# Two-layer attention and GEGLU kernel with a planned instruction order: last unit in two parts of keys, fillers near both ends, new constants per stretch

## The chip, the cores and the metric

The kernel runs on one NeuronCore of one Trainium2 chip. The metric is the device time in microseconds (us), the median of the runs shown. There are five engines with queues of their own: TensorE (PE, matmuls; its weight loads are a separate row, PEld), VectorE (DVE), ScalarE (ACT), GpSimd (POOL) and SyncE (SP, which only issues DMAs here). SBUF is the working memory, PSUM the accumulators: 8 banks of 512 fp32 columns on 128 partitions.

## The reference

Two rounds of the same two layers, on x of 2048 tokens by 512, in bfloat16. LN is a layernorm without parameters, H = 32 heads of 16:

```python
x = x + A(LN(x));  x = x + B(LN(x));  x = x + A(LN(x));  x = x + B(LN(x))
# A: q, k, v = split_heads(x @ wqkv)
#    o = softmax(q @ k.T * 16 ** -0.5) @ v ;  merge_heads(o) @ wo
# B: (gelu_tanh(x @ w_gate) * (x @ w_up)) @ w_down      # w_gate, w_up: 512 x 1792
```

## The kernel before, in words

Everything stays in SBUF between load and store. Queries are worked in blocks, 512,512,512,512 in the first layer and 512,512,512,256,256 in the second (`layer_blocks`). A *unit* is one block for one group of 4 heads, so there are 8 units per block. For each unit:

- **Phase 1** (`p1_emit`, matmul L1507): scores of 128 queries by 512 keys for one head, four heads in four row groups of the array; DVE reduces each such tile, or two banks at once, to the row maximum (L1522, banks 0 to 3). Some tiles are *folded*: a matmul against a difference of two key blocks, an ACT relu (L1334), and one DVE operation (L1517) do two tiles in one. `fin` makes the negative maximum of all keys, transposes it (L897, L899), and `negmax` puts it by four small DMAs (L916, SP's queue) into a spare row of the query tile in `QT`, so that the second matmul has the maximum already subtracted.
- **Phase 2** (`p2_emit`, matmul L1378): scores again, transposed, 512 columns a tile. ACT takes the exponential (L1354) out of banks 4 to 6 (also 3 in the wide mode), two banks at once (128x1024, a *pair*) or one (128x512, a *single*), into a slot of `SCR`. Then the products with V (`pv_emit`, L1402) accumulate in bank 7; `nrm` divides by the sum.
- Beside these run the projections and the feed-forward (L651), transposes (L749), their evictions (L666 DVE, L668 ACT), out-projection with the residual (L979 DVE or L984 ACT + POOL), gelu (L1091 ACT), the up product (L1104 DVE or L1110 ACT + POOL), and the last sum and store (L1130).

The order on every engine is fixed when the program is built. A planner keeps a reckoned clock for each engine (`clk`) and, at each step of PE, takes phase 1, phase 2, products, or other work (`chains`, by due time). Its choices hang on 19 constants that change every 16 steps of phase 1 (`PLAN`, one line of constants per stretch, 129 lines). Three matter for reading the change:

- `NT`: how many banks of phase 2 are issued in one go. `P2B`: whether phase 2 outside the wide mode may use a pair: 0 singles only (banks 4, 5, 6), 1 a pair in 4 and 5 and a single in 6, 2 pairs at 4 or 5. `LAG`: how far phase 2 may trail phase 1 before the wide mode.
- Fillers: `warm_emit` (L1544) issues a matmul of zeros, 240 columns, whose result nobody reads. [...]

The first three units of the second layer (`split`) are worked in two parts already: exponentials of 12 of 16 key tiles with the maximum of those keys, kept (`keep_part`), scaled by exp of the difference of the maxima, and added to the rest (`nrm`).

The last unit of all is an ordinary one before: its `nrm` takes the quick path (L941, L943), straight out of bank 7. After it come the out-projection of the last 256 rows, their layernorm (`ln_fast`), their feed-forward and the store; the other engines have nothing else left then.

Of the kernel before, what the change touches and what calls it, by code (L numbers as in the profile page):

```python
# [6 lines left out]
BF = mybir.dt.bfloat16  # L7
F32 = mybir.dt.float32
# [12 lines left out]
PLAN = [  # L21
# [289 lines left out]
def _build(nc, x_in, wqkv, wo, wg, wu, wd, out, layer_blocks=((512, 512, 512, 512), (512, 512, 512, 256, 256)),  # L311
# [16 lines left out]
    with es:  # L328
# [267 lines left out]
        for la in range(1, NL):  # L596
            for i, u in enumerate([u for u in range(NU) if units[u][0] == la][:NSPL]):
                assert units[u][3] == 512 and i < n_pre
                split[u] = i
# [1169 lines left out]
```

## Time and profile before

| | |
|---|---|
| median of 3 runs | 2550.32 us (2549.87 to 2550.61) |
| the profiled execution: its own time | 2550.05 us |
| its span, first to last instruction | 2548.3 us |
| busy in the span | PE 2450.2, DVE 2423.5, ACT 2356.9, POOL 589.6 us |
| granted PE clock, mean | 0.999 |

Three views are used. The page gives busy time per engine, the chain of waits that ended last, and groups of instructions (count, busy us, mean ns of one, then idle time of the engine in front of them and what ended it). The windows give busy time of every engine between two times, then the granted clock and the DMA share. The timeline gives runs of equal instructions in order, with the idle time in front of them in square brackets.

### The profile page before, as it was taken

The page shows a single profiled execution, that of the slowest core. Times are in us where ns is not written, and L with a number is a line of the kernel's source. Part 1 is how long each engine was busy: PE and PEld are TensorE (multiplying, and loading weights), DVE is VectorE, ACT ScalarE, POOL GpSimd, SP SyncE. Part 2 cuts the span into 40 slices and gives each one's busy share as a digit, 9 for nine tenths or more (in the row PEclk, how much of TensorE's full clock was granted, in tenths as well). Part 3 has the DMA queues.
Part 4 walks back from the last instruction along what each step waited for, and adds up shares of the span by engine and source line. Part 5 has one row for each costly group of instructions (what it writes and reads, how often), then busy time and mean ns, then how long its engine had stood idle before and what let it go on. Part 6 is the DMA issues. An engine that isn't in the chain of part 4 may idle for free.

```text
span 2548.3 us, 67924 instructions
## 1 busy us (share of the span) xinstructions
PE 2450.2 (96%) x29939; PEld 1166.4 (46%) x29939; DVE 2423.5 (95%) x3191; ACT 2356.9 (92%) x3111; POOL 589.6 (23%) x722
## 2 busy tenths in 40 slices
PE   7999999999999999999999999999999999999998
PEld 3444443444434454444434455444543445544555
DVE  7999999999999999999998999999999999999993
ACT  7899998999989999999979899999998999989996
POOL 4010123311133213421133211241113211341200
PEclk9999999999999999999999999999999999999999
DMA  3110000000000000000000000000000000000000
GB/s 100 38 56 6 4 8 2 4 2 2 8 2 4 4 2 6 4 2 16 10 5 4 12 2 4 8 4 8 5 8 1 6 6 3 4 3 12 3 7 6
DMA packets 27367, 25.04 MB, mean 10 GB/s; under 512 B 9408, under 2 KB 26048, under 8 KB 27072
## 3 DMA queue, kind: packets, MB, share of 16 engines
q1 hardware_dynamic: 27072, 20.71, 2.8%
q8 instruction: 234, 3.83, 0.6%
q14 instruction: 61, 0.50, 0.1%
HBM read 9.70 MB, written 2.10 MB: 5 GB/s over the span
## 4 chain that ended last, share of the span: by engine, by line
PE 43%; ACT 32%; DVE 23%; issue 1%; POOL 0%; POOLq 0%; ACTq 0%
ACT SCR L1354 29%; DVE PM L1522 22%; PE PS L1507 14%; PE PS L651 12%; PE PS L1402 9%; PE PS L1378 4%; PE PS L1544 4%; ACT SCR L1334 1%; DVE SCR L1517 1%; PE PS L1327 1%; PE PS L749 0%; ACT XNT L668 0%; ACT SG L668 0%; ACT AO L984 0%; ACT ACCS L948 0%
## 5 line engine op out<-in xcount | busy, mean ns | idle before, releaser
L1522 DVE TENSOR_REDUCE PM<-PS 128x1 f32<-128x512 f32 (+1 forms) x2492 | 2207.6, 948 | 56.2 <-PE PS L1378 27.8
L1354 ACT ACTIVATE SCR<-PS 128x1024 bf16<-128x1024 f32 (+1 forms) x2385 | 2002.7, 931 | 72.4 <-PE PS L1378 51.2
L1507 PE MATMUL PS<-KT,QT 32*128 32x512 bf16 x3914 | 1008.2, 384 | 40.0 <-DVE PM L1522 25.2
L1378 PE MATMUL PS<-QT,KT 32*128 32x512 bf16 (+1 forms) x4608 | 926.3, 360 | 14.0 <-ACT SCR L1354 11.9
L1402 PE MATMUL PS<-VP,SCR 128*128 128x51 bf16 (+1 forms) x16384 | 808.9, 187 | 18.2 <-ACT SCR L1354 13.3
L1402 PEld LDWEIGHTS PS<-VP,SCR 128*128 128x128 bf16 x16384 | 571.0, 96 | 509.7 <-issue 427.1
L1507 PEld LDWEIGHTS PS<-KT,QT 32*128 32x128 bf16 x3914 | 240.8, 91 | 514.7 <-DVE PM L1522 298.2
L1544 PE MATMUL PS<-WV,ZER 128*128 128x240 bf16 x2483 | 432.3, 266 | 4.1 <-ACT SCR L1354 4.1
L966 POOL TENSOR_TENSOR RL<-ACCS,CM 128x16 f32<-128x16 f32 (+1 forms) x63 | 173.4, 2753 | 1032.8 <-ACT ACCS L948 1032.5
L1378 PEld LDWEIGHTS PS<-QT,KT 32*128 32x128 bf16 x4608 | 228.9, 91 | 85.7 <-ACT SCR L1354 62.5
L1544 PEld LDWEIGHTS PS<-WV,ZER 128*128 128x128 bf16 x2483 | 189.0, 96 | 67.9 <-issue 53.9
L1112 POOL TENSOR_TENSOR HT<-HT,AO 128x512 bf16<-128x512 bf16 (+1 forms) x109 | 121.2, 1113 | 273.7 <-ACT AO L1110 273.7
L651 PE MATMUL PS<-WD,HT 128*128 128x512 bf16 x448 | 130.6, 381 | 0.1
L651 PE MATMUL PS<-XNT,WU 128*128 128x512 bf16 (+1 forms) x504 | 127.6, 357 | 0.0
L1517 DVE CUSTOM_DVE_ANT_0 SCR<-PS,SCR 128x512 bf16<-128x512 f32 x182 | 118.0, 685 | 6.0 <-PE PS L1507 2.3
L1149 POOL TENSOR_TENSOR KD<-KT 128x512 bf16<-128x512 bf16 x71 | 81.9, 1154 | 176.1 <-PE PS L1327 162.2
L651 PE MATMUL PS<-XNT,WG 128*128 128x512 bf16 (+1 forms) x504 | 119.4, 359 | 1.3 <-ACT HT L1091 0.9
L1091 ACT ACTIVATE HT<-PS 128x512 bf16<-128x512 f32 (+1 forms) x126 | 69.1, 550 | 50.5 <-PE PS L651 49.5
L1334 ACT ACTIVATE SCR<-PS 128x1024 bf16<-128x1024 f32 (+1 forms) x116 | 99.3, 856 | 16.1 <-PE PS L1327 15.6
L986 POOL TENSOR_TENSOR X<-X,AO 128x512 f32<-128x512 f32 x46 | 58.3, 1268 | 197.2 <-ACT AO L984 197.0
L1110 ACT ACTIVATE AO<-PS 128x512 f32<-128x512 f32 (+1 forms) x109 | 63.8, 585 | 0.4
L651 PEld LDWEIGHTS PS<-XNT,WG 128*128 128x128 bf16 x504 | 39.2, 98 | 53.5 <-issue 29.3
(99 smaller groups left out, 884.9 us busy)
## 6 DMA issues: line engine op xcount, KB each, us to landing
KT<-SG SPq DMA_DIRECT2D x64, 64.0 KB
QT<-MT SPq DMA_DIRECT2D x236, 1.0 KB
QT<-SG SPq DMA_DIRECT2D x56, 64.0 KB
out_dram<-AO SPq DMA_DIRECT2D x16, 128.0 KB, 1.7
WG<-in_B_w_gate_dram SPq DMA_DIRECT2D x4, 448.0 KB, 5.1
WU<-in_B_w_up_dram SPq DMA_DIRECT2D x4, 448.0 KB, 4.8
WD<-in_B_w_down_dram SPq DMA_DIRECT2D x4, 384.0 KB, 4.9
SCR<-in_A_x_dram SPq DMA_DIRECT2D x2, 512.0 KB, 5.4
```

What stands on the lines that cost most here:

```text
L651: ins = e.matmul(out_ap, lhsT=l, rhs=r_, start=(i == 0), stop=(i == n - 1))
L966: emit("pool", lambda e: e.tensor_tensor(RL[:, s, 0:4 * nq], lsum, CM1[:, 0:4 * nq], op=ALU.pow), r=[("ACCS", s), ("CM1",)], w=[("RL", s)] ...
L1112: emit("pool", lambda e, ft=ft, o=o: e.tensor_tensor(HT[:, ft, 0:n], HT[:, ft, 0:n], AO[:, o, 0:n], op=ALU.mult), r=[("AO", o), ("HT", ft) ...
L1149: emit("pool", lambda e: e.tensor_tensor(KD[:, s, :], KT[:, g, ka * 512:(ka + 1) * 512], KT[:, g, kb * 512:(kb + 1) * 512], op=ALU.subtrac ...
L1334: emit("act", lambda e: e.activation(PT[:, s0:s0 + cnt, :], PS[:, bk:bk + cnt, :], ACTF.Relu), r=bks, w=[("PT", s0 + d) for d in range(cnt ...
L1354: emit("act", lambda e: e.activation(dst, src, ACTF.Exp, scale=DH ** -0.5), r=[BK[bk + i] for i in range(cnt)], w=[("PT", i) for i in slot ...
L1378: ins = e.matmul(bank(bk)[:, i * n:(i + 1) * n], lhsT=KT[32 * j:32 * j + 32, g, kt * 128:(kt + 1) * 128], rhs=QT[32 * j:32 * j + 32, s, 0: ...
L1402: ins = e.matmul(acc, lhsT=PT[:, slot, i * n + qt * 128:i * n + (qt + 1) * 128], rhs=AP(VP, (kt * H + 4 * g + j) * 17, [[NTT * H * 17, 128 ...
L1507: ins = e.matmul(bank(b), lhsT=QT[32 * j:32 * j + 32, s, qt * 128:(qt + 1) * 128], rhs=KT[32 * j:32 * j + 32, g, kb * 512:(kb + 1) * 512], ...
L1517: emit("dve", lambda e, i=i, b=b, sl=sl: e.tensor_tensor_reduce(PT[:, sl, :], bank(b), PT[:, sl, :], 1.0, -3.0e38, ALU.add, ALU.max, po[:, ...
L1522: emit("dve", lambda e: e.tensor_reduce(po, PS[:, bs[0]:bs[0] + cnt, :], axis=AX.X, op=ALU.max), r=bks, w=[("PM", sm) + h[1:] for h in hs] ...
L1544: return e.matmul(PS[:, b, NACC:512], lhsT=ZER[:, :], rhs=WV[:, 0, 0:512 - NACC], start=(b != 7), stop=(b != 7), skip_group_check=True)
```

## The change

- **PLAN**: 120 of the 129 lines of constants differ. `NT` is 3 in 39 lines (11 before), `P2B` is 0 in 24 (8 before).
- **TSPL**: the last unit (256 queries) goes into `split` too: part one is keys 0 to 1535 (`TNA` = 3 of 4 blocks), part two the rest. Its phase 1 list is sorted by part. The first part has a query tile of its own (`q_copy`, POOL) with the partial maximum; `keep_part`, the scale (`merge`) and one DVE addition in `nrm` join the parts. The same switch for the first unit (HSPL) is off.
- **merge**: the scaling of a kept part, which stood in `nrm`, becomes a chain of its own that may run earlier; phase 1 of the unit six later also waits for it.
- **TW**: once no phase 2 and no products are left, fillers are wanted up to an occupancy of 0.95 instead of 0.55.
- **HF**: in the first 60 us of the planner's clock, from 12 us on, gaps of PE are filled with fillers whatever the occupancy.

Counted in the two programs' order: PE fillers 2483 to 2408; exponentials: pairs 1711 to 1575, singles 674 to 946; relus of folds: pairs 66 to 53, singles 50 to 79; folds 182 to 185; DVE maxima: pairs 1240 to 1237, singles 1252 in both.

```diff
 PLAN = [
-    (0.0, 0.15, 0.45, 0.42, 0.3, -0.05, 1, 1, 62, 84, 8, 60, 0.3, 2.0, 0, 2, 2, 2, 7),
+    (0.0, 0.25, 0.45, 0.42, 0.3, -0.05, 1, 1, 70, 84, 8, 60, 0.3, 2.0, 0, 2, 2, 2, 7),
...
-NSPL=3, VS=14,
+NSPL=3, HSPL=0, TSPL=1, HNA=3, TNA=3, HV=16, TW=0.95, HF=60, VS=14,
...
+        if TSPL:
+            assert units[NU - 1][3] <= 256
+            split[NU - 1] = NSPL
+            n_part[NU - 1] = TNA
+            extra[NU - 1] = NU % n_qt
+            tail = [h for h in p1_list if h[0] == NU - 1]
+            p1_list[len(p1_list) - len(tail):] = [h for h in tail if h[2] < TNA] + [h for h in tail if h[2] >= TNA]
...
+        def merge(u):
...
+            yield ("cond", lambda: u in kept and u in fin_rec and gel["on"] is None)
+            yield ("pool", [("MSEL", s1), ("MSB", i)], [("DW", i)])
+            emit("pool", lambda e: e.tensor_tensor(DW[:, i, 0:4 * nq], sgn[0], sgn[1], op=ALU.subtract),
...
+            yield ("act", [("DW", i)], [("DW", i)])
+            emit("act", lambda e: e.activation(DW[:, i, 0:4 * nq], DW[:, i, 0:4 * nq], ACTF.Exp, scale=DH ** -0.5),
...
+            emit("pool", lambda e: e.tensor_tensor(pv, pv, wv, op=ALU.mult),
...
+        def q_copy(u):
...
+            emit("pool", lambda e: e.tensor_copy(QT[:, s2, 0:n], QT[:, sl, 0:n]), ...
...
         def nrm(u):
...
             if FAST and (SF or la == NL - 1) and t0 + n == S and g == NG - 1:
+                src, src_t, src_o, keys = PS, 8 * 512, 7 * 512, [BK[7]]
+                if u in split:
+                    av = ACCS[:, s, 0:na].rearrange("p (a b) -> p a b", a=nq)
+                    emit("dve", lambda e: e.tensor_tensor(av, PS[:, 7, 0:na].rearrange("p (a b) -> p a b", a=nq), pa, op=ALU.add),
+                         r=[BK[7]] + pk, w=[("ACCS", s)], dur=0.1 + 0.067 * nq)
+                    src, src_t, src_o, keys = ACCS, 2 * NACC, s * NACC, [("ACCS", s)]
...
-            if u >= n_ahead and u - n_ahead not in qp2_rec:
+            if u >= n_ahead and (u - n_ahead not in qp2_rec or u - n_ahead in split and u - n_ahead not in merged):
                 return None
...
             want, must = (WARM + BOOST, WARML + BOOST / 2) if ahead else (WARM, WARML)
+            if TW and p2["u"] >= NU and not pvq:
+                want = must = TW
             cool = load < want and now > 12 and warm_bank(now) is not None
...
+            if HF > now > 12 and mode[0] == "full" and est(r=[("WV",)], w=[BK[7]]) <= now:
+                for _ in range(int((tn - now - 0.1) / 0.105)):
+                    sch.op("pe", warm_fn(7), r=[("ZER",), ("WV",)], w=[BK[7]])
             clk["pe"] = max(now + 0.01, tn)
```

More of the change, by code (lines that the diff above doesn't have):

```diff
@@ L595, in _build @@
         split = {}
+        n_part = {}
+        extra = {}
         for la in range(1, NL):
@@ L599, in _build @@
                 split[u] = i
+                n_part[u] = NKB - 1
+        if HSPL:
+            split[0] = 0
+            n_part[0] = HNA
+            extra[0] = n_qt - 1
+        if TSPL:
[5 more added lines that the diff above has]
+            p1_list[len(p1_list) - len(tail):] = [h for h in tail if h[2] < TNA] + [h for h in tail if h[2] >= TNA]
         seq = []
@@ L603, in _build @@
                 seq.append((u, 2))
-            elif split[u] == 0:
-                seq += [(v, pt) for pt in (0, 1) for v in sorted(split) if units[v][0] == units[u][0]]
+            elif split[u] in (0, NSPL):
+                seq += [(v, pt) for pt in (0, 1) for v in sorted(split) if v == u or u not in extra and units[v][0] == units[u][0] and v not in extra]
         first_p1 = {}
@@ L614, in _build @@
         p1_left = {u: 16 * units[u][3] // 128 for u in range(NU)}
-        p1_part = {u: 12 * units[u][3] // 128 for u in split}
+        p1_part = {u: 4 * n_part[u] * units[u][3] // 128 for u in split}
         part_rec = set()
         part_done = set()
+        copied = set()
+        kept = set()
+        merged = set()
+        merges = {}
         pair = {u: (2, 3) if u == 0 else (0, 1) for u in range(NU)}
@@ L839, in qproj @@
                 yield ("cond", lambda: u + 1 - n_qt in p2_done)
+            if 0 in extra and u + 1 == extra[0]:
+                yield ("cond", lambda: 0 in part_done)
             tts = range(t0 // 128, (t0 + n) // 128)
@@ L854, in fn @@
                     return ins
-                emit("sp", fn, r=[("SG", s), ("ZER",)], w=keys, grp="sd%d" % (2 * s + i), nd=2 if u + i >= n_qt else 1, dur=0.3)
+                emit("sp", fn, r=[("SG", s), ("ZER",)], w=keys, grp="sd%d" % (2 * s + i), nd=2 if u + i >= n_qt or 0 in extra and u + i == extra[0] else 1, dur=0.3)
                 qt1_rec.add(u + i)
@@ L906, in negmax @@
             s1 = u % n_ahead
-            sl = u % n_qt
+            sl = extra[u] if part and u in extra else u % n_qt
             nq = units[u][3] // 128
-            if u in split and not part:
+            if u in extra:
+                yield ("cond", lambda: u in copied)
+            elif u in split and not part:
                 yield ("cond", lambda: u in part_done)
@@ L925, in part_out @@
             i = split[u]
+            if i == NSPL:
+                return ATT[:, 2:2 + units[u][3] // 128, 0:136].bitcast(F32), [("ATTX",)]
             lo = (0, 192, 328)[i]
@@ L1180, in _build @@
         for la in range(NL):
+            u0 = min(u for u in range(NU) if units[u][0] == la)
             for b in range(NKB):
@@ L1188, in _build @@
                     due = first_k[(la, 2 * c, b)] - KD_
-                    if b == NKB - 1 and any(units[u][0] == la and units[u][4] // 2 == c for u in split):
-                        due = min(due, blk_end[units[min(split)][1] - 1] + VS - 1)
+                    if b == NKB - 1 and la and any(units[u][0] == la and units[u][4] // 2 == c for u in split if u not in extra):
+                        due = min(due, blk_end[units[u0][1] - 1] + VS - 1)
                     add(kproj(la, c, b), due, True)
-            u0 = min(u for u in range(NU) if units[u][0] == la)
             for tt in range(NTT):
-                if u0 in split:
+                if u0 in split and u0 not in extra:
                     add(vproj(la, tt), blk_end[units[u0][1] - 1] + VS)
                 else:
-                    add(vproj(la, tt), last_p1[u0] + VD + 2 * tt)
+                    add(vproj(la, tt), last_p1[u0] + VD + 2 * tt - (HV if u0 in extra and tt < 4 * n_part[u0] else 0))
             for bi, (bl, qi, t0, n) in enumerate(blocks):
@@ L1208, in _build @@
                 add(qproj(u), first_p1[u] - QD, True)
+        for u in extra:
+            add(q_copy(u), first_p1[u])
         if FMAX:
@@ L1216, in _build, with kgs @@
         pvq = []
-        part_kg = {0: (0, NTT - 4), 1: (NTT - 4, NTT)}
-        pv_left = {(u, pt): 4 * (NTT if pt == 2 else part_kg[pt][1] - part_kg[pt][0]) * units[u][3] // 512 for u, pt in seq}
+        def kgs(u, pt):
+            a = 4 * n_part[u] if pt < 2 else 0
+            m = 512 // units[u][3]
+            return list(range(a // m if pt == 1 else 0, a // m if pt == 0 else NTT // m))
+        pv_left = {(u, pt): 4 * len(kgs(u, pt)) for u, pt in seq}
         pv_first = set(seq)
@@ L1224, in p2_group @@
                 return None
-            if seq[p2["i"]][1] == 0 and any(vp_rec.get(kt) != units[u][0] for kt in range(NTT - 4)):
+            if seq[p2["i"]][1] == 0 and any(vp_rec.get(kt) != units[u][0] for kt in range(4 * n_part[u])):
                 return None
@@ L1228, in p2_group, with q_slot @@
                 pt = seq[p2["i"]][1]
-                p2["todo"] = [list(range(*part_kg[pt]) if pt < 2 else range(NTT * units[u][3] // 512)) for j in range(4)]
+                p2["todo"] = [kgs(u, pt) for j in range(4)]
             return u
+        def q_slot(u):
+            return extra[u] if u in extra and seq[p2["i"]][1] == 0 else u % n_qt
         def p2_left():
@@ L1277, in f_head @@
             u = i[0]
-            if u not in kd_rec or u not in qt1_rec or (u >= n_ahead and u - n_ahead not in qp2_rec):
+            if u not in kd_rec or u not in qt1_rec or (u >= n_ahead and (u - n_ahead not in qp2_rec or u - n_ahead in split and u - n_ahead not in merged)):
                 return None
@@ L1449, in p1_skip @@
                 p1_left[u] -= 1
-                if u in split:
+                if u in split and p1_list[pos["g"]][2] < n_part[u]:
                     p1_part[u] -= 1
+                    assert p1_part[u]
                 pos["p1"] += 0.5
@@ L1463, in p1_plan @@
                 return None
-            if u >= n_ahead and u - n_ahead not in qp2_rec:
+            if u >= n_ahead and (u - n_ahead not in qp2_rec or u - n_ahead in split and u - n_ahead not in merged):
                 return None
-            if u in split and kb == NKB - 1 and u not in part_rec:
+            if u in split and u not in extra and kb >= n_part[u] and u not in part_rec:
                 return None
@@ L1526, in p1_emit @@
             p1_left[u] -= cnt
-            if u in split and hs[0][2] < NKB - 1:
+            if u in split and hs[0][2] < n_part[u]:
                 p1_part[u] -= cnt
```

89 lines of the change are left out of this document (57 added, 32 removed), and 233 rows, old and new, of the table PLAN.

## The prediction, made before the changed kernel ran

> **What bounds the kernel now.** I read the page's busy shares first, then its chain, then windows cut at the kernel's own stages, then the groups by shape, and the timeline where an edit lands.
>
> ```profile
> PE 2450.2 (96%) x29939; PEld 1166.4 (46%) x29939; DVE 2423.5 (95%) x3191; ACT 2356.9 (92%) x3111; POOL 589.6 (23%) x722
> PE 43%; ACT 32%; DVE 23%; issue 1%; POOL 0%; POOLq 0%; ACTq 0%
> ```
>
> No engine has much room: DVE works 95% of the span and ACT 92%, and the chain that ends last changes between PE, ACT and DVE all the time. PE's own share is mostly the hand-over between an eviction and the next one. So the kernel is bound by two engines that alternate, and time can only come from their idle time. Where that lies, the windows say (columns: length, then busy of PE, PEld, DVE, ACT, POOL, then clock):
>
> ```profile
> 0.00:60.00 60.00, 47.12 (x242) 18.83 (x242) 43.30 (x63) 46.76 (x90) 27.02 (x59) 1.00 0.36 106
> 60.00:1280.00 1220.00, 1178.23 (x14483) 557.12 (x14483) 1195.26 (x1587) 1155.65 (x1495) 271.63 (x333) 1.00 0.03 9
> 1280.00:1420.00 140.00, 137.51 (x1257) 54.45 (x1256) 124.74 (x182) 116.59 (x177) 45.77 (x64) 1.00 0.03 7
> 1420.00:2440.00 1020.00, 988.61 (x12613) 477.67 (x12611) 994.97 (x1264) 955.44 (x1244) 241.41 (x260) 1.00 0.02 5
> 2440.00:2493.00 53.00, 51.06 (x830) 27.86 (x828) 51.64 (x67) 51.50 (x62) 2.25 (x4) 1.00 0.02 5
> 2493.00:2516.00 23.00, 21.70 (x329) 12.09 (x328) 1.02 (x4) 22.30 (x28) 0.40 (x1) 1.00 0.01 2
> 2516.00:2549.00 33.00, 26.02 (x199) 18.41 (x199) 12.54 (x29) 8.65 (x19) 1.12 (x2) 0.93 0.02 8
> ```
>
> Between 60 and 2493 us DVE is idle 24.7 + 15.3 + 25.0 + 1.4 = 66 us and ACT 64.4 + 23.4 + 64.6 + 1.5 = 154 us. The rest of DVE's idle time is the head (17 us) and the two last stages (42 us). In 2493 to 2516 ACT alone works (22.3 of 23 us): the exponentials of the end. So whatever the constants do, they cannot win more than about 66 us in the middle while DVE's work stays as it is, and a gain of 20 us already asks for a third of DVE's idle time there.
>
> **The constants: what the new order costs.** The two programs' order gives the counts. DVE's maxima are 3 pairs fewer and 3 folds more, so its work stays within about 2 us. ACT's changes: 136 pairs of exponentials become 272 singles.
>
> ```profile
> L1354 ACT ACTIVATE SCR<-PS 128x1024 bf16<-128x1024 f32 x1711 | 1664.4, 1059 | 63.3 <-PE PS L1378 46.0 <-PE PS L1507 1.9 <-issue 0.2
> L1354 ACT ACTIVATE SCR<-PS 128x512 bf16<-128x512 f32 x674 | 407.6, 606 | 9.1 <-PE PS L1378 5.2
> 2441.25 1.51 ACT L1354 ACTIVATE SCR<-PS 128x1024 bf16<-128x1024 f32 x2 [0.20 <-PE PS L1378]
> 2442.97 1.51 ACT L1354 ACTIVATE SCR<-PS 128x1024 bf16<-128x1024 f32 x2 [0.21 <-PE PS L1378]
> 2448.42 7.35 ACT L1354 ACTIVATE SCR<-PS 128x1024 bf16<-128x1024 f32 x8 [0.48 <-PE PS L1378]
> 2455.67 0.28 ACT L948 ACTIVATE ACCS<-PS 128x136 f32<-128x136 f32 x1
> ```
>
> The first two rows are groups (count, busy, mean ns, idle in front). The four others are the timeline. Eight pairs in a row take 2455.67 - 2448.42 = 7.25 us, 0.906 us each from start to start, less than their mean length of 1.059: each starts before the one in front has ended. A pair and a single in turn (the rows with x2) take 2442.97 - 2441.25 = 1.72 us for three tiles, and 0.2 us of that is a wait for PE, which cannot refill the pair's two banks while ACT reads them. That wait is where pairs lose: 46.0 us of their idle time is put down to L1378, against 5.2 for singles.
>
> No stage of this trace runs singles in three banks, so their start to start is bounded. From below it is half a pair, 0.453 us; from above the mean length, 0.606, with no overlap. At 0.453 the 272 singles cost 272 x 0.453 - 136 x 0.906 = 0 us of ACT; at 0.606, 164.8 - 123.2 = +42 us. I take 0.50, because the pair shows an overlap of 1.059 - 0.906 = 0.15 us that a single should share in most part: +13 us. The folds' relus (29 singles more, 13 pairs fewer) add 29 x 0.50 - 13 x 0.906 = 3 us, and the added evictions (three transposes, three 256-column copies) some 3 us. Against these +19 us of work stands the wait: 136 of the hand-overs of 0.21 us are 29 us less idle. On ACT alone that is about -10 us, and it only counts where ACT, not DVE, is the late one.
>
> [...]
>
> The second reading of the constants is the fillers. A filler goes in when the planner finds PE under 0.55 occupied. For the same real matmuls, fewer fillers mean fewer such gaps. Between the head's extra fillers and the last maximum the order has 2401 of them before and 2274 after, 127 fewer (the 21 new ones of the head and those after the last phase 1 tile, 82 before and 113 after, are left out).
>
> ```profile
> L1544 PE MATMUL PS<-WV,ZER 128*128 128x240 bf16 x2483 | 432.3, 266 | 4.1 <-ACT SCR L1354 4.1
> 2509.53 0.41 PE PS L1544 x4
> 2525.79 1.00 PE PS L1544 x5
> ```
>
> Four of them took 0.41 us on the chain, 0.103 each. So 127 are 13 us of PE less. If the rule of 0.55 held everywhere, each filler missing stands for 0.103/0.55 us of gap: 23 us. That is the upper end for what was aimed at, and zero the lower end if chip and planner do not agree to a tenth of a microsecond. I take -16 us for the middle of the kernel, near the middle of 13 and 23 with something off for that disagreement, and consistent with the -10 us found on ACT plus what DVE gets from it.
>
> **The last unit in two parts.** In the trace of before the last unit does not wait for its maximum:
>
> ```profile
> 2492.29 0.39 PE L1507 MATMUL PS<-KT,QT 32*128 32x512 bf16 x1
> 2493.68 0.21 DVE L899 STREAM_TRANSPOSE MT<-MSEL 128x32 bf16<-128x32 bf16 x1
> 2501.30 3.91 ACT L1354 ACTIVATE SCR<-PS 128x1024 bf16<-128x1024 f32 x4
> 2505.69 10.20 ACT L1354 ACTIVATE SCR<-PS 128x1024 bf16<-128x1024 f32 x13 [0.48 <-PE PS L1378]
> L916 SPq DMA_DIRECT2D QT<-MT x20: 520/521/534, 2412.1 to 2495.6; - x20
> 2516.37 0.21 DVE L941 RECIPROCAL RL<-PS 128x8 f32<-128x8 f32 x1 [14.59 <-PE PS L1402]
> 2516.61 0.29 DVE L943 TENSOR_TENSOR ATT<-PS,RL 128x128 bf16<-128x128 f32 x1
> 2516.95 0.62 PE L749 MATMUL PS<-IDN,ATT 128*128 128x128 bf16 x8 [0.32 <-DVE ATT L943]
> ```
>
> Its maximum is transposed at 2493.9 and its DMAs are issued until 2496.1, but ACT only gets to it at 2501.3, as it still works on the unit before. So the split takes no wait away. What it allows is that phase 2 follows phase 1 more closely: after the last phase 1 matmul 46 tiles of phase 2 stand in the order before, 38 after. ACT's last 13 instructions here are 7 pairs and 6 singles, 20 tiles in 10.2 us, 0.51 a tile. Eight tiles are -4.1 us. Against it: the last 20 tiles are singles now (at 0.50, -0.2; at 0.606, +1.9); a kept copy and the factor's exponential on ACT, of the size of L948's 0.28 us each, +0.5; and one DVE addition between last product and reciprocal, as long as L943, +0.3. Sum: -4.1 - 0.2 + 0.5 + 0.3 = -3.5 with singles at 0.50, -1.4 at 0.606; I take -2.5, between them. POOL's query copy, subtraction and scale, and SP's four DMAs more (4 x 0.52 = 2.1 us of issuing), lie under the 38 tiles of exponentials that come after them (17 us and more at 0.453 a tile), with only the partial maxima's own DMAs queued behind them on SP. If that cover went, the second part would wait up to 2.1 us.
>
> **Fillers at the end and at the head.** After the last product 72 fillers stand in the order instead of 27, 23 of them between the layernorm's two transposes.
>
> ```profile
> 2521.00:2522.00 1.00, 0.00 (x0) 0.00 (x0) 0.61 (x3) 0.00 (x0) 0.24 (x1) 1.00 0.00 0
> 2524.00:2525.00 1.00, 0.68 (x4) 0.18 (x2) 0.42 (x1) 0.00 (x1) 0.55 (x1) 0.50 0.00 0
> 2522.97 0.40 PE L749 MATMUL PS<-IDN,XN 128*128 128x128 bf16 x4 [2.31 <-DVE XN L686]
> 2523.20 1.47 PE L1544 MATMUL PS<-WV,ZER 128*128 128x240 bf16 x10
> 2525.18 0.61 PE L749 MATMUL PS<-IDN,XN 128*128 128x128 bf16 x4 [0.51 <-DVE XN L686]
> 2526.58 6.67 PE L651 MATMUL PS<-XNT,WG 128*128 128x256 bf16 x56
> 2533.09 6.28 PE L651 MATMUL PS<-XNT,WU 128*128 128x256 bf16 x56
> ```
>
> PE stands still for 2.31 us here, and a little later its granted clock is 0.50. The second transposes take 0.61 us where the first took 0.40, and the gate product 6.67 where the equal up product took 6.28. Keeping the clock up is worth 0.2 + 0.4 = 0.6 us. But 23 fillers at 0.103 are 2.4 us in a gap of 2525.18 - 2523.20 = 2.0 us, so the second transposes may come 0.4 us late. I take 0, with -0.6 to +0.6 as ends. At the head 21 fillers may lift the clock sooner:
>
> ```profile
> 13.82 1.89 PE L651 MATMUL PS<-WV,XNT 128*128 128x512 bf16 x4 [0.69 <-DVE XNT L666]
> 19.79 1.04 PE L651 MATMUL PS<-XNT,WQ 128*128 128x512 bf16 x4 [0.69 <-ACT XNT L668]
> ```
>
> Four projections take 1.89 us there and 1.04 five microseconds later. One such group sooner at full speed is -0.85 us; three fillers in front of a ready matmul are +0.3. I take 0, as ACT and POOL set the pace of these loads' layernorms. `merge`, for the three units of the layer seam, moves the same few small operations earlier and costs nothing: they lie on POOL, busy 589.6 of 2548.3 us.
>
> **The sum.** Against the profiled execution's own 2550.05 us (median of the runs 2550.32, so the same): -16 - 2.5 + 0 + 0 = 2531.5 us.
>
> **The rivals.**
> - *The constants do not carry over.* They were fitted to a reckoned clock, and a new order is only better where chip and reckoning agree to some 0.1 us per hand-over. Against: the pair's 0.906 us is what the planner reckons (0.055 + 2 x 0.4267 = 0.908). Then only the tail's -2.5 to 0 remain: 2547.5 to 2550. Chance 0.10.
> - *ACT becomes the bound (slower).* Place: the stretches that now run phase 2 in singles, most of all the 128 phase 1 tiles from the 3584th on, with 112 singles and 20 pairs in the order after, 37 and 57 before. A single that does not overlap the one before it costs 0.606 and waits for PE like the pair does: 42 + (29 x 0.606 - 13 x 0.906 = 6) + 3 = 51 us more of ACT with no wait saved. ACT holds 32% of the chain: 51 x 0.32 = +16, less 2.5 for the tail: 2563.5. It decides from a start to start above 0.534 us, where 301 x 0.534 - 135 + 3 equals the 29 us of waits. For it: no stage shows 0.50. Against: the overlap of pairs. Chance 0.12. [...]
> - *The clock drops.* With 127 fillers fewer, a stretch could fall to 0.50 as at 2524 us. Ten fillers then took 1.47 instead of 1.03 us; over the 3 us of such a drop PE loses about 1.5 us, and 14 drops would eat the gain: about 2552 to 2556. Against: the clock is 1.00 in all windows up to 2516 and the 0.55 rule is unchanged. Chance 0.03.
> - *More than forecast.* DVE's idle time in the middle halves, 66 to 33 us: 2550 - 33 - 2.5 = 2514.5. Chance 0.12.
>
> **How the numbers follow.** The forecast (2522 to 2543: the middle between -5 and -25) has 0.63. A measurement of this kernel can tell about 0.2%, 5.1 us, from no change. Faster by more: 0.63 + 0.12 + 0.03 of the first rival = 0.78. Within: 0.07 of the first rival and 0.01 of the third = 0.08. Slower: 0.12 + 0.02 = 0.14. The range takes in the larger gain with the tail's ends and the first rival, and leaves out most of the two slower ones: 2512 to 2552.
>
> **What would show it right or wrong.** Right: DVE's idle time between 60 us and its last maximum near 50 us instead of 66, ACT's near 120 instead of 154 with ACT's busy sum up by 15 to 25; runs of singles at about 0.50 us from start to start; ACT's wait for L1378 clearly under 51 us; the stretch from the last phase 1 matmul to the first transposes of the out-projection 2 to 3 us shorter than 2492.3 to 2516.95; no clock of 0.50 in the tail. Wrong: singles that follow each other at 0.6 us or more, ACT idle time that stays at 154 us, or a gain that sits in the head or the tail rather than between.

## The result, and the profile after

| | before | after |
|---|---|---|
| median | 2550.32 us of 5 runs (2549.07 to 2552.24) | 2538.18 us of 5 runs (2537.47 to 2542.37) |
| profiled execution: own time, span | 2550.05, 2548.3 us | 2542.32, 2540.6 us |
| ratio to before | | 0.9958, 95% interval 0.9943 to 0.9972 |

The changed kernel is 12.1 us faster by the medians; 18.8 were forecast. Its five times fall on two values: 2537.47, 2537.80 and 2538.18 us at a mean clock of 1.000, 2542.32 and 2542.37 at 0.998. The profile caught one of the latter, in which the granted clock of PE is 0.50 for 10.24 us near the end, so its last 55 us are read beside an experiment's below.

The page after, its busy row and its chain:

```profile
PE 2434.9 (96%) x29660; PEld 1170.1 (46%) x29864; DVE 2421.7 (95%) x3192; ACT 2371.5 (93%) x3270; POOL 591.8 (23%) x743
PE 43%; ACT 29%; DVE 26%; issue 1%; POOL 0%; ACTq 0%
```

ACT's share of the chain fell from 32 to 29% and DVE's rose from 23 to 26%: the chain moved to the engine that had less room from the start. The windows of after are cut at the same points of the work as those of before (columns as there):

```profile
0.00:60.00 60.00, 47.97 (x256) 20.51 (x261) 43.01 (x62) 46.73 (x90) 27.07 (x59) 1.00 0.35 106
60.00:1276.00 1216.00, 1166.94 (x14344) 555.63 (x14437) 1195.03 (x1590) 1157.71 (x1508) 270.84 (x344) 1.00 0.03 9
1276.00:1416.00 140.00, 136.28 (x1212) 54.57 (x1231) 123.36 (x183) 118.17 (x185) 45.77 (x67) 1.00 0.03 8
1416.00:2433.00 1017.00, 981.65 (x12548) 477.83 (x12633) 996.32 (x1261) 969.97 (x1376) 244.84 (x265) 1.00 0.02 5
2433.00:2486.00 53.00, 51.70 (x821) 27.52 (x820) 50.60 (x67) 52.27 (x65) 1.21 (x3) 1.00 0.02 4
2486.00:2508.00 22.00, 21.50 (x262) 11.95 (x259) 1.23 (x6) 18.03 (x31) 0.98 (x3) 0.81 0.01 2
2508.00:2541.00 33.00, 28.90 (x231) 22.14 (x230) 12.15 (x28) 8.67 (x19) 1.13 (x2) 0.97 0.03 9
```

Between 60 us and the last maximum ACT is idle 58.3 + 21.8 + 47.0 + 0.7 = 127.8 us, 26 less than before, and busy 2298.1, 18.9 more. DVE is idle 21.0 + 16.6 + 20.7 + 2.4 = 60.7 us, only 5.7 less than its 66.4. The last maximum comes 7.5 us earlier, which is DVE's idle time (some 5.7) and its work (some 1.8), not ACT's 26. The groups by shape say the same; first two rows of before, then four of after:

```profile
L1522 DVE TENSOR_REDUCE PM<-PS 128x2 f32<-128x1024 f32 x1240 | 1493.7, 1217 | 39.7 <-PE PS L1378 19.0 <-PE PS L1507 12.0 <-PE PS L1327 0.4
L1522 DVE TENSOR_REDUCE PM<-PS 128x1 f32<-128x512 f32 x1252 | 842.9, 682 | 16.5 <-PE PS L1378 8.8 <-PE PS L1507 2.2 <-PE PS L1327 1.7
```

```profile
L1594 DVE TENSOR_REDUCE PM<-PS 128x2 f32<-128x1024 f32 x1237 | 1491.9, 1219 | 37.9 <-PE PS L1449 17.3 <-PE PS L1579 9.0 <-PE PS L1398 0.2
L1594 DVE TENSOR_REDUCE PM<-PS 128x1 f32<-128x512 f32 x1252 | 844.3, 683 | 13.9 <-PE PS L1449 6.0 <-PE PS L1579 2.0 <-PE PS L1398 0.7
L1425 ACT ACTIVATE SCR<-PS 128x1024 bf16<-128x1024 f32 x1575 | 1534.3, 1068 | 40.2 <-PE PS L1449 27.7
L1425 ACT ACTIVATE SCR<-PS 128x512 bf16<-128x512 f32 x946 | 550.4, 610 | 17.6 <-PE PS L1449 11.8
```

(L1522 of before is L1594 of after, L1354 is L1425, L1378 is L1449, L1507 is L1579, L1544 is L1618.) ACT's waits for the matmuls of phase 2 went from 46.0 + 5.2 to 27.7 + 11.8 us, while the idle time in front of the maxima went from 39.7 + 16.5 to 37.9 + 13.9.

The end, by the timeline: the last maximum transposed, the join of the two parts, the reciprocal; then ACT's exponentials, of which the 18 are 4 pairs and 14 singles.

```profile
2486.16 0.21 DVE L952 STREAM_TRANSPOSE MT<-MSEL 128x32 bf16<-128x32 bf16 x1
2507.24 0.30 DVE L1007 TENSOR_TENSOR ACCS<-PS,ATT 128x136 f32<-128x136 f32 x1 [17.47 <-PE PS L1473]
2507.58 0.20 DVE L1010 RECIPROCAL RL<-ACCS 128x8 f32<-128x8 f32 x1
2489.35 11.14 ACT L1425 ACTIVATE SCR<-PS 128x1024 bf16<-128x1024 f32 x18
2501.30 1.57 ACT L1425 ACTIVATE SCR<-PS 128x512 bf16<-128x512 f32 x3 [0.55 <-PE PS L1449]
2503.36 0.60 ACT L1425 ACTIVATE SCR<-PS 128x512 bf16<-128x512 f32 x1 [0.48 <-PE PS L1449]
2504.37 0.60 ACT L1425 ACTIVATE SCR<-PS 128x512 bf16<-128x512 f32 x1 [0.41 <-PE PS L1449]
```

From the last maximum's transposition to the reciprocal it is 2507.6 - 2486.4 = 21.2 us here (22.5 before), and from there to the end 33.0 (31.9 before). ACT waits 0.4 to 0.55 us in front of three of its last singles. They fall into a half clock, as windows of 3.4 us each show (PE busy, then the clock):

```profile
2496.10:2499.50 3.40, 3.40 (x40) 1.00 0.02 5
2499.50:2502.90 3.40, 3.40 (x30) 0.51 0.00 0
2502.90:2506.30 3.40, 3.40 (x31) 0.50 0.00 0
2506.30:2509.70 3.40, 3.40 (x23) 0.50 0.00 0
```

Half clock from 2499.5 to 2509.8, 10.24 us. The same stretch at full clock is in the fourth experiment, and with that the 12.1 us can be told apart: 7.5 up to the last maximum, 4.4 from there to the reciprocal, little after it.

### The profile page after: what moved, and what is told of

The parts are those of the page before. It is cut to its first block, busy times and chain, and to the rows that moved or that the text cites. A ratio compares the mean times of both kernels' runs of the same rounds, so it can differ in the third digit from the quotient of the medians.

```text
span 2540.6 us, 67774 instructions
## 1 busy us (share of the span) xinstructions
PE 2434.9 (96%) x29660; PEld 1170.1 (46%) x29864; DVE 2421.7 (95%) x3192; ACT 2371.5 (93%) x3270; POOL 591.8 (23%) x743
## 4 chain that ended last, share of the span: by engine, by line
PE 43%; ACT 29%; DVE 26%; issue 1%; POOL 0%; ACTq 0%
ACT SCR L1425 27%; DVE PM L1594 25%; PE PS L1579 13%; PE PS L670 11%; PE PS L1473 9%; PE PS L1449 4%; PE PS L1618 4%; ACT SCR L1405 1%; PE PS L1398 1%; PE PS L768 0%; DVE SCR L1589 0%; ACT AO L1045 0%; ACT XNT L687 0%; ACT ATTT L687 0%; ACT ACCS L1017 0%
## 5 line engine op out<-in xcount | busy, mean ns | idle before, releaser
L1594 DVE TENSOR_REDUCE PM<-PS 128x1 f32<-128x512 f32 (+1 forms) x2489 | 2204.7, 949 | 51.9 <-PE PS L1449 23.3
L1425 ACT ACTIVATE SCR<-PS 128x1024 bf16<-128x1024 f32 (+1 forms) x2521 | 2017.5, 896 | 57.8 <-PE PS L1449 39.5
L1579 PE MATMUL PS<-KT,QT 32*128 32x512 bf16 x3911 | 1006.4, 384 | 36.2 <-DVE PM L1594 19.4
L1449 PE MATMUL PS<-QT,KT 32*128 32x512 bf16 (+1 forms) x4608 | 940.0, 360 | 11.5 <-ACT SCR L1425 8.5
L1579 PEld LDWEIGHTS PS<-KT,QT 32*128 32x128 bf16 x3911 | 240.3, 91 | 506.9 <-DVE PM L1594 286.6
L1618 PE MATMUL PS<-WV,ZER 128*128 128x240 bf16 x2408 | 425.9, 267 | 7.7 <-ACT SCR L1425 6.9
L1449 PEld LDWEIGHTS PS<-QT,KT 32*128 32x128 bf16 x4608 | 232.7, 91 | 89.8 <-ACT SCR L1425 60.5
L1618 PEld LDWEIGHTS PS<-WV,ZER 128*128 128x128 bf16 x2408 | 184.6, 97 | 73.7 <-issue 53.0
L1405 ACT ACTIVATE SCR<-PS 128x512 bf16<-128x512 f32 (+1 forms) x132 | 103.7, 786 | 23.5 <-PE PS L1398 23.2
L670 PE MATMUL PS<-XNT,WU 128*128 128x512 bf16 (+1 forms) x444 | 116.4, 354 | 6.6 <-issue 5.5
L670 PE MATMUL PS<-WD,HT 128*128 128x512 bf16 x378 | 114.3, 380 | 8.0 <-issue 6.5
```

The lines of the kernel that those rows point to most:

```text
L670: ins = e.matmul(out_ap, lhsT=l, rhs=r_, start=(i == 0), stop=(i == n - 1))
L1405: emit("act", lambda e: e.activation(PT[:, s0:s0 + cnt, :], PS[:, bk:bk + cnt, :], ACTF.Relu), r=bks, w=[("PT", s0 + d) for d in range(cnt ...
L1425: emit("act", lambda e: e.activation(dst, src, ACTF.Exp, scale=DH ** -0.5), r=[BK[bk + i] for i in range(cnt)], w=[("PT", i) for i in slot ...
L1449: ins = e.matmul(bank(bk)[:, i * n:(i + 1) * n], lhsT=KT[32 * j:32 * j + 32, g, kt * 128:(kt + 1) * 128], rhs=QT[32 * j:32 * j + 32, s, 0: ...
L1579: ins = e.matmul(bank(b), lhsT=QT[32 * j:32 * j + 32, s, qt * 128:(qt + 1) * 128], rhs=KT[32 * j:32 * j + 32, g, kb * 512:(kb + 1) * 512], ...
L1594: emit("dve", lambda e: e.tensor_reduce(po, PS[:, bs[0]:bs[0] + cnt, :], axis=AX.X, op=ALU.max), r=bks, w=[("PM", sm) + h[1:] for h in hs] ...
```

## The experiments

In the times below, "last maximum" is the end of its transposition and "reciprocal" the start of the last one on DVE, both of the profiled execution. Before has 2493.9, 2516.4 and its end at 2548.3 us.

**The constants alone, and the rest alone.** The first kernel is the changed one with the split and both filler rules off (`merge` stays a chain of its own in it, and was not tried by itself), the second has the old constants under the new code.

```diff
-TSPL=1, HNA=3, TNA=3, HV=16, TW=0.95, HF=60
+TSPL=0, HNA=3, TNA=3, HV=16, TW=0, HF=0
```

> The new constants without the three edits near the ends (last unit whole, no extra fillers at head or end). Theory C: the constants carry the change. They bring the last phase 1 matmul forward by some 7.5 us (2492.7 to 2485.2 in the two profiles) and leave 38 instead of 46 tiles of phase 2 after it, 8 x 0.5 = 4 us: 2538 to 2540 us, and since 70 fillers instead of 41 stand between the last phase 1 matmul and the last product, the clock of 0.50 that the changed kernel's profile shows from 2499.5 to 2509.8 us is absent in all runs. Rival S: the end's part of the gain comes from the split and its fillers; then only the middle's gain is left, 2542 to 2543 us.

```diff
-PLAN = [ ...new, 129 lines... ]
+PLAN = [ ...as before, 129 lines... ]
```

> The old constants with the three edits near the ends. Theory C: the split takes no wait away, its 46 tiles after the last phase 1 matmul stay; the fillers around the last layernorm keep the clock and bring at most 0.6 us, the joining costs 0.3 to 0.8: 2549.5 to 2551 us. Rival S: the end's gain of 4.7 us seen without the clock drop is here: 2545 to 2546 us.

Constants alone: 2539.68 us, 0.9964 of before [0.9952, 0.9977]. Old constants with all the rest: 2551.65 us, 1.0004 [0.9996, 1.0013]. The timelines of DVE, first of the constants alone, then of the old constants:

```profile
2484.32 0.21 DVE L952 STREAM_TRANSPOSE MT<-MSEL 128x32 bf16<-128x32 bf16 x1
2506.64 0.21 DVE L1010 RECIPROCAL RL<-PS 128x8 f32<-128x8 f32 x1 [19.18 <-PE PS L1473]
```

```profile
2494.88 0.21 DVE L952 STREAM_TRANSPOSE MT<-MSEL 128x32 bf16<-128x32 bf16 x1
2517.94 0.20 DVE L1010 RECIPROCAL RL<-ACCS 128x8 f32<-128x8 f32 x1
```

The constants bring 10.7 of the 12.1 us (before took 2550.43 us beside them), and most of it up to the last maximum (2484.5 against 2493.9, 9.4 us); the stretch to the reciprocal is 22.1 us, nearly as long as before. The long half clock was expected to be absent in all runs of this kernel, but two of the twelve took 2547.01 and 2556.65 us at mean clocks of 0.996 and 0.992. Where these fell, no trace shows. The rest on the old constants brings nothing: last maximum 1.2 us later, 22.8 us to the reciprocal. In that order ACT gets to the last unit long after its maximum is ready, so there is nothing for the split to take away.

**No split; no fillers at the end.**

```diff
-TSPL=1
+TSPL=0
```

> The changed kernel with the last unit whole. Theory C: 38 tiles are left after the last phase 1 matmul here too, the unit's maximum is ready long before ScalarE gets to it, and 70 fillers instead of 41 stand in the last unit's stretch: all runs near 2537 us, none at 2542. Rival S: without the split ScalarE waits for the maximum at the end, 2541 to 2542 us.

2540.75 us, 0.9959 [0.9945, 0.9973], all five runs at a clock of 1.000 (2540.22 to 2541.14). The timeline of ACT, then of DVE, then one row of PE:

```profile
2487.14 0.28 ACT L1017 ACTIVATE ACCS<-PS 128x136 f32<-128x136 f32 x1 [0.47 <-PE PS L1473]
2489.73 11.34 ACT L1425 ACTIVATE SCR<-PS 128x1024 bf16<-128x1024 f32 x17 [2.31 <-PE PS L1449]
2484.53 0.21 DVE L952 STREAM_TRANSPOSE MT<-MSEL 128x32 bf16<-128x32 bf16 x1
2506.84 0.21 DVE L1010 RECIPROCAL RL<-PS 128x8 f32<-128x8 f32 x1 [19.17 <-PE PS L1473]
2486.95 2.42 PE L1618 MATMUL PS<-WV,ZER 128*128 128x240 bf16 x22
```

Here ACT stands still for 0.47 + 2.31 = 2.8 us after the last maximum. With the new constants it has by then done nearly all of the unit before, so the last unit's maximum is late, and with the split, whose first part does not need it, that wait is gone. The theory that the split does nothing fell. How much of the wait the maximum itself asks for is not shown: the planner filled it with the 22 fillers, and phase 2 stands behind them on PE. The 38 tiles are there without the split, so they come from the constants.

```diff
-TW=0.95
+TW=0
```

> The changed kernel with 26 instead of 72 fillers after the last product. Theory C: the clock drop in the last unit lies before these fillers and stays in some of the runs, so two times some 4.6 us apart, each 0.5 to 1 us over the changed kernel's (2538.3 and 2543); the profile shows a clock of 0.50 for about 3.4 us after the layernorm's gap, as before. Rival: the fillers make no difference or delay the transposes, then the same times or up to 0.5 us less.

2537.12 us, 0.9944 [0.9932, 0.9957], runs 2535.02 to 2538.09. Up to the reciprocal this kernel issues the same order as the changed one, and no run fell below a mean clock of 0.999. Its timelines: DVE, ACT (again 4 pairs and 14 singles, then the last 6), PE; then its windows where the changed kernel lost its clock.

```profile
2485.78 0.21 DVE L952 STREAM_TRANSPOSE MT<-MSEL 128x32 bf16<-128x32 bf16 x1
2504.14 0.20 DVE L1010 RECIPROCAL RL<-ACCS 128x8 f32<-128x8 f32 x1
2500.24 3.06 ACT L1425 ACTIVATE SCR<-PS 128x512 bf16<-128x512 f32 x6
2510.74 0.40 PE L768 MATMUL PS<-IDN,XN 128*128 128x128 bf16 x4 [2.31 <-DVE XN L705]
2512.96 0.40 PE L768 MATMUL PS<-IDN,XN 128*128 128x128 bf16 x4 [0.80 <-DVE XN L705]
```

```profile
2495.70:2499.10 3.40, 3.40 (x40) 1.68 (x38) 0.00 (x0) 3.33 (x8) 0.00 (x0) 1.00 0.00 0
2499.10:2502.50 3.40, 3.40 (x44) 1.79 (x42) 0.00 (x0) 3.40 (x10) 0.42 (x1) 1.00 0.02 5
```

At full clock the stretch from last maximum to reciprocal is 2504.1 - 2486.0 = 18.1 us, 4.4 less than before and 4.0 less than without the split; the last maximum itself comes 1.3 us later than without it, so the split is worth 2.7 us at the reciprocal and about 3 in the time (2540.75 to 2537.8). The six last singles follow one another without a wait, (3.06 - 0.61)/5 = 0.49 us from start to start. The fillers between the transposes, in the changed kernel:

```profile
2515.59 0.40 PE L768 MATMUL PS<-IDN,XN 128*128 128x128 bf16 x4 [0.67 <-DVE XN L705]
2515.83 2.52 PE L1618 MATMUL PS<-WV,ZER 128*128 128x240 bf16 x23
2518.18 0.39 PE L768 MATMUL PS<-IDN,XN 128*128 128x128 bf16 x4
```

With the 23 fillers the second transposes start 2.59 us after the first, without them 2.22: 0.37 us late, and no wait is left in front of them. In this execution the clock held without the fillers too (1.00 from 2486 to 2536 us), and it takes 31.3 us from the reciprocal to the end.

**Fillers in the last unit.** Once phase 1 is done, fillers up to an occupancy of 0.8; 76 stand there instead of 41.

```diff
             if TW and p2["u"] >= NU and not pvq:
                 want = must = TW
+            elif pos["g"] >= len(p1_list):
+                want, must = 0.8, 0.55
```

> The changed kernel with more fillers once phase 1 is done (76 instead of 41 between the last phase 1 matmul and the last product). Theory H (too little work on TensorE in the last unit lets its clock fall in some runs): no run at 2542, all near 2537.8 or up to 1 us more for fillers in front of ready matmuls; the profile has a clock of 1.00 from 2486 to 2508 us. Rival (the drop has another cause, such as an outside throttle): the two times 2537.8 and 2542.3 stay, in about the same share of the runs.

2539.23 us, 0.9956 [0.9944, 0.9969], all five at 1.000 (2538.44 to 2539.58). No half clock in its profile (1.00 from 2486 to 2536 us), but its reciprocal comes 19.7 us after its last maximum where 18.1 are possible. So these fillers cost about 1.5 us (1.6 in the trace, 1.4 against 2537.8). Whether they are what held the clock is less sure: the kernels with the last unit of the changed one (it, the one without end fillers, and three below) fell to a mean of 0.998 or less in 4 of 24 runs, and at that rate none in five would be nothing rare. From the reciprocal to the end it is 31.7 us here, with all end fillers and at full clock.

**The pairs back, new order otherwise.** `P2B` 1 in the 24 lines where it is 0.

```diff
-    (0.1, 0.1, 0.55, 0.42, 0.3, -0.15, 1, 0, 22, 84, 8, 60, 0.3, 2.0, 0, 2, 4, 1, 9),
+    (0.1, 0.1, 0.55, 0.42, 0.3, -0.15, 1, 1, 22, 84, 8, 60, 0.3, 2.0, 0, 2, 4, 1, 9),
```

> The changed kernel with pairs allowed again in the 24 stretches that forbade them (1734 pairs and 811 singles in all of ScalarE's tiles, against 1628 and 1025). Theory P (singles are what lets phase 2 keep up near the end): the order leaves 62 instead of 38 tiles of phase 2 after the last phase 1 matmul, 24 x 0.46 = 11 us, and the middle moves by 1 us (DVE's maxima cost 1 us more): 2548 to 2551 us. Rival Q (singles only cost ScalarE time): 2537 or less.

2549.18 us, 0.9996 [0.9986, 1.0005]: the whole gain gone, but none of it in the middle. A window up to its last maximum, two groups and the timeline:

```profile
60.00:2484.00 2424.00, 2356.21 (x28963) 1110.73 (x28964) 2364.43 (x3093) 2280.78 (x3017) 562.48 (x677) 1.00 0.03 8
L1425 ACT ACTIVATE SCR<-PS 128x1024 bf16<-128x1024 f32 x1682 | 1642.5, 1067 | 62.2 <-PE PS L1449 47.4 <-PE PS L1579 0.3
L1425 ACT ACTIVATE SCR<-PS 128x512 bf16<-128x512 f32 x732 | 443.5, 607 | 8.8 <-PE PS L1449 5.6
2485.27 0.21 DVE L952 STREAM_TRANSPOSE MT<-MSEL 128x32 bf16<-128x32 bf16 x1
2516.03 0.20 DVE L1010 RECIPROCAL RL<-ACCS 128x8 f32<-128x8 f32 x1
```

ACT's waits for phase 2 are back at 47.4 + 5.6 = 53 us, and yet the last maximum is at 2485.5, no later than in the changed kernel (0.9 us earlier, one trace of each); DVE is idle 59.6 us, against 60.7. The singles bring the last maximum no earlier. What they bring shows at the end: with pairs 62 tiles of phase 2 stand behind the last phase 1 tile instead of 38, and the stretch to the reciprocal is 30.6 us instead of 18.1.

**Half of the new constants.** Lines 0 to 64 new and the rest old, then the reverse.

```diff
+PLAN = PLAN_NEW[:65] + PLAN_OLD[65:]      # and the other: PLAN_OLD[:65] + PLAN_NEW[65:]
```

> New constants in the first 64 stretches, old ones after, the edits near the ends kept. Theory M (the middle's gain lies in both layers, 4.5 us at the seam of the layers and 3 us after it, and the end's needs the last stretches' constants): 2551.65 - 4.5 = 2547 us, with 46 tiles left after the last phase 1 matmul. Theory F (each filler missing between the ends is worth 7.5 us / 127 = 0.06 us): 2390 against 2425 fillers with the old constants, -2 us: 2549.5 us. Theory D (VectorE's own work decides: 28 more single maxima, 9 fewer pairs and 5 fewer folds than in the changed kernel, +3.5 us): the last phase 1 matmul 3.5 us later than in the changed kernel, 2487.7.

> Old constants in the first 64 stretches, new ones after, the edits near the ends kept. Theory M: without the first layer's 4.5 us, with the second's 3 us and the end's 5 us: 2543 us. Theory F: 2373 against 2295 fillers between the ends in the changed kernel, 78 x 0.06 = 4.7 us: 2542.5 us. Theory D: 20 fewer single maxima, 15 more pairs, 5 fewer folds, +2 us: 2540 us. If the constants only suit the order that they were fitted to, the second half's gain is gone as well: 2547 us.

New first half: 2564.6 us, 1.0056 [1.0042, 1.007], slower than before, where every theory of its text had a gain. New second half: 2548.66 us, 0.9999 [0.999, 1.0008]; three of its ten runs took 2553.5 to 2553.8 us at a mean clock of 0.998. The first half's window to its last maximum, a group of it, and its timeline; then the timeline of the second half's:

```profile
60.00:2506.00 2446.00, 2373.31 (x29128) 1118.68 (x29128) 2377.09 (x3122) 2280.05 (x2986) 548.50 (x659) 1.00 0.03 8
L1165 DVE TENSOR_TENSOR HT<-PS,HT 128x512 bf16<-128x512 f32 x11 | 7.5, 683 | 0.1
2507.66 0.21 DVE L952 STREAM_TRANSPOSE MT<-MSEL 128x32 bf16<-128x32 bf16 x1
```

```profile
2496.49 0.21 DVE L952 STREAM_TRANSPOSE MT<-MSEL 128x32 bf16<-128x32 bf16 x1
2514.85 0.20 DVE L1010 RECIPROCAL RL<-ACCS 128x8 f32<-128x8 f32 x1
```

With the new first half the first layer is as quick as in the changed kernel, 4 to 5 us ahead of before between 1200 and 1290 us. Then it loses 19 us under the old constants and ends 14 behind before, most of that as work: up to its last maximum, 1.9 us after that window, DVE is busy 2379 us instead of 2367, as the planner hands it among others eleven up products of 512 columns, 7.5 us, a shape that DVE does not have in before. The new second half behind the old first has its last maximum 2.8 us later than before, and gains only at the end (18.2 us to the reciprocal). So the 7.5 us are no sum of what each half is worth: about -5 + 2.8 would be about -2.

**One line of 129.** Line 2, one price, old in the changed kernel and new in before.

```diff
-    (0.0, 0.15, 0.45, 0.42, 0.3, -0.05, 1, 1, 62, 84, 8, 60, 0.3, 2.0, 0, 2, 2, 2, 7),
+    (0.1, 0.15, 0.45, 0.42, 0.3, -0.05, 1, 1, 62, 84, 8, 60, 0.3, 2.0, 0, 2, 2, 2, 7),
```

> The changed kernel with one of its 129 lines of constants (line 2, of layer 1; one price, 0.0 to 0.1) as before. Tiles left after the last maximum: 38 as in the changed kernel, fillers 14 more in the middle. Theory 'the constants are fitted to one order, and a shift early on changes what comes after': the last maximum moves by 2 to 8 us later, 2540 to 2546. Rival 'the new constants are better line by line': one line of 129 is worth 0.1 us of the 7.5, so the time is within 1 us of 2538.2.

> The kernel before with the same one line as in the changed kernel (0.1 to 0.0). Theory 'fitted to one order': the last maximum moves by 1 to 6 us, later rather than earlier, 2551 to 2556. Rival 'better line by line': within 1 us of the kernel before, 2549.3 to 2551.3.

Old line in the changed kernel: 2540.40 us, 0.9962 [0.9948, 0.9975], runs 2538.19, 2539.72, 2541.09 and 2544.36, the last at a clock of 0.997. Its last maximum is at 2486.6, 0.2 later. New line in before: 2550.59, 1.0002 [0.9993, 1.0012], ten runs of which the slowest took 2556.13 us at 0.996, last maximum at 2494.6, 0.7 later. Neither moved it by the 2 to 8 or 1 to 6 us that the theory "fitted to one order" asked for. But the old line's median, 2.2 us above the changed kernel's, lies where that theory had it (2540 to 2546) and not within the rival's 1 us; its trace is that of its fastest run, so this stays undecided. In the old kernel a difference of one line stays local: the order comes together again, and after the first 150 of 3914 phase 1 matmuls the kernel with the new line stays 0.5 to 0.9 us behind to the end. In the changed kernel it does not: the order with the old line has two phase 1 matmuls and 14 fillers more.

**Fewer fillers.** Two versions meant to beat the changed kernel.

```diff
-TW=0.95, HF=60
+TW=0, HF=0          # and the other: TW=0.75, HF=0
```

> The changed kernel without its fillers between the transposes at the end (TW=0) and without those that go into the last block regardless of occupancy (HF=0); 26 filler matmuls are left after the last maximum beside the 41 of the last unit. Theory 'both filler rules cost a little and buy nothing': the second transposes come at the end 2.2 us after the first instead of 2.6, as with TW=0 alone, the end of the chain moves by nothing more, and the median is 2536.5 to 2537.5. Rival 'the fillers hold the clock': a stretch of half clock appears in the last block and the time is 2540 or more.

> The changed kernel with TW=0.75 and HF=0, so 41 filler matmuls at the end in the place of 72 (all) and 26 (none). Theory 'both filler rules cost a little and buy nothing': between the two, 2536.8 to 2538. Rival 'the fillers hold the clock': the clock at the end stays whole, as with all of them, and the transposes aren't late: 2535 to 2536.5.

(The first text places the fillers of `HF` in the last block; the code puts them in the first 60 us.) None: 2537.36 us, 0.9947 [0.9934, 0.9959], runs 2536.11 to 2537.76. 0.75: 2538.37 us, 0.9952 [0.9939, 0.9964], runs 2536.42 to 2541.45, the slowest at a clock of 0.997. Without `TW` alone it was 2537.12. So all three are within a microsecond of the changed kernel at full clock (2537.8), and none is shown to beat it. Without any, two runs at a clock of 1.000 took 2536.1 and 2536.3 us, three at 0.999 took 2537.4 to 2537.8. What a fall of the clock costs the traces show better than these times, as runs of one kernel at full clock lie up to 2 us apart (2535.0 to 2537.1 without `TW`). The constants alone, which have no `TW` either, had one in the tail; their windows, then one without `TW` alone:

```profile
2513.00:2514.00 1.00, 0.76 (x7) 0.66 (x7) 0.97 (x3) 0.16 (x1) 0.00 (x0) 0.66 0.00 0
2514.00:2515.00 1.00, 1.00 (x8) 0.74 (x5) 0.30 (x2) 0.44 (x1) 0.55 (x1) 0.50 0.00 0
2515.00:2516.00 1.00, 1.00 (x9) 0.80 (x7) 0.40 (x1) 0.00 (x0) 0.00 (x0) 0.50 0.00 0
2516.00:2517.00 1.00, 1.00 (x9) 0.70 (x7) 0.00 (x0) 0.60 (x1) 0.00 (x0) 0.63 0.00 0
```

```profile
2508.00:2536.00 28.00, 21.16 (x167) 15.53 (x165) 10.68 (x25) 6.57 (x16) 1.13 (x2) 1.00 0.03 10
```

The half clock of the first lasts some 3.4 us, from 2513.3 to 2516.7, and from the reciprocal to the end it takes 31.7 us; before, with one of 3.41 us, takes 31.9. Without `TW`, at a clock of 1.00, it is 31.3, so a fall of this length costs 0.4 to 0.6 us. With all fillers at full clock it was 31.7, so every run pays about 0.4 us for them: about what such a fall costs.

## Why the prediction was right, and where its sum was not

**The side and the place were right.** The gain lies up to the last maximum and in the tail, and the rivals did not come: the constants carried over, ACT did not become the bound, and the clock did not fall in the middle (1.00 in every window up to 2486).

**The middle, -16 forecast, -7.5 measured: the mis-sized term.** ACT's sums came near the forecast: 18.9 us more busy for the 19 forecast (some 4 of them are the eight tiles that now come before the last maximum), idle time down to 127.8 for "near 120". But the wait that was to bring this fell by less. "136 of the hand-overs of 0.21 us" were 29 us; the waits for phase 2 went from 51.2 to 39.5, "clearly under 51" and yet only 12 less. The larger part came from a place that the prediction does not name, the gelus, while the relus of the folds wait longer (16.1 to 23.5 us). The gelus before, after and with the pairs put back:

```profile
L1091 ACT ACTIVATE HT<-PS 128x512 bf16<-128x512 f32 (+1 forms) x126 | 69.1, 550 | 50.5 <-PE PS L651 49.5
L1152 ACT ACTIVATE HT<-PS 128x512 bf16<-128x512 f32 (+1 forms) x126 | 69.1, 550 | 31.8 <-PE PS L670 29.3
L1152 ACT ACTIVATE HT<-PS 128x512 bf16<-128x512 f32 (+1 forms) x126 | 69.0, 550 | 32.9 <-PE PS L670 31.5
```

So that ACT's idle time fell by about as much as forecast is in part luck. The failed step is the one behind it, "consistent with the -10 us found on ACT plus what DVE gets from it". DVE got 5.7 us of idle time, not 16 (60.7 for "near 50"). The pairs put back show why: ACT's waits for phase 2 return, those of the gelus do not, and the last maximum stays where it is. So in the middle ACT has room, and its waits for phase 2 are hidden behind DVE. What gives DVE its 5.7 us is not shown. The other support, 127 fillers fewer as 13 to 23 us (24 by its own figures), fell with it: a filler tells where the planner reckoned a gap, not what the chip lost. The pairs put back have 19 fillers more than the changed kernel between 60 us and the last phase 1 matmul, and their last maximum is no later; the new first half has 30 fewer than before there (2357 against 2387), and its last maximum is 14 us later.

**Pairs against singles.** A single costs more per tile, 0.49 us against 0.45 for half a pair. Yet with singles ACT, which the middle does not fill, has 38 tiles left at the end and not 62, and that is the 12 us by which the pairs put back are late there, where DVE is done and ACT's backlog alone counts.

**Singles at 0.50 us from start to start.** 0.49 measured, so the bound of 0.606 and with it the slower rival are out. The trace of before could have told: in nine places of it a single follows a single without idle time, most often after 0.48 or 0.49 us.

**The tail, -2.5 forecast.** -4.4 at full clock, -1.3 in the profiled execution. "The split takes no wait away" was read from the trace of before and holds for its constants (2551.65 us with the old ones). Under the new ones it does not: ACT reaches the last unit before its phase 2 can start, and with the split 2.8 us of waiting are gone. The 8 tiles are the constants' and are worth nothing without it: 22.1 us with 38 tiles and no split, 22.5 before with 46. What was forecast as the cover of POOL's and SP's added work held: at full clock no wait stands in front of the second part.

**The fillers, 0 forecast.** Close: `TW` makes the second transposes 0.37 us late, as worked out (0.4). A half clock of 3.4 us costs 0.4 to 0.6 us by the traces (0.6 reckoned), and only in the runs that have one; that the fillers hold the clock was the author's estimate, and no run shows it. At the head the row of projections that was to show a sooner full clock is unchanged, 1.89 us as before, and the granted clock is 1.00 over it in both traces (13.8 to 15.7 us), so a slower clock that fillers could lift is not shown there:

```profile
13.84 1.89 PE L670 MATMUL PS<-WV,XNT 128*128 128x512 bf16 x4 [0.69 <-DVE XNT L685]
```

**"No clock of 0.50 in the tail"** was wrong for the traced run, 0.50 from 2499.5 to 2509.8, and by its mean clock of 0.998 for one more of the five; the place was not the one watched.

**What stays open.** Which of the 120 lines bring the 9.4 us of the constants alone up to the last maximum, and by what: it is not the singles. That the halves cannot be exchanged is shown for one cut, through the work which the planner then hands to DVE; that every line depends on those before it is not, and the one line tried leaves it undecided.

## What to carry to other kernels

Of two engines that are nearly full, price a change by the idle time of the fuller one, and count a wait saved on the other as nothing until a run shows that it is late: here ACT had 26 us less idle time and the last maximum of DVE came 7.5 us earlier, and giving 15 of the 26 back did not make it later. At the end of the program it is the other way round, since one engine's backlog is all that is left there, and an edit can be worth nothing with one order and 3 us with another, so measure it together with the order that it is meant for. A planner's own marks, such as its count of fillers, show what the planner believed and not what the chip lost.

## What the runs showed of the hardware

In the traced run of the changed kernel PE's granted clock halved right after a stretch in which PE, by the modelled ends of its matmuls, had not stood still. In the window from 2496.1 to 2499.5 PE was busy for 3.40 of 3.40 us with 40 matmuls and the clock was 1.00; in the next, to 2502.9, it was 0.51. The kernel without end fillers ran the same 40 in its window from 2495.7 to 2499.1, also busy for 3.40 us, and its clock was 1.00 there and in the next. What made the difference the runs do not show.

The half clock lasted 10.24 us in this run, 3.41 us in the trace of before (from 2524.0) and some 3.4 us in that of the constants alone (from 2513.3). In these two PE had stood still shortly ahead of it, for 2.31 us in before and some 2.3 us in the constants alone; in the kernel without end fillers it stood still for 2.31 us up to 2510.74, and the clock was 1.00 from 2508 to 2536. The half clock of 10.24 us is worth 4.5 us: 2542.3 against 2537.8.
